# Attention and two expert layers on one core: the tokens of the smaller experts in two steps of four experts side by side instead of five steps of one

## The chip, the cores and the metric

The kernel runs on one core of one Trainium2 chip. The metric is the device time of one execution in microseconds (us); lower is better. The kernel before takes 847.58 us (median of three runs, 847.08 to 849.77).

## The reference

Three layers follow each other. All data are fp32.

```python
out_g = softmax(scale * q_g @ k_all.T) @ v_all        # 32 global tokens see all
out_l = softmax(global + windowed local scores) @ v   # 512 local tokens, window 32
x = concat(out_g, out_l) -> (4 * 544, 8 * 64) = (2176, 512)

h = x @ w_in                                          # 512 -> 2048
g = where(h >= 1, h, where(h <= -1, 0, (h + 1) ** 2 / 4))
x = g @ w_out                                         # 2048 -> 512

logits = normalised(x) @ normalised(expert_emb).T / tau      # 8 experts
expert_idx = argmax(logits); gate = softmax(logits)[expert_idx]
out[n] = gate[n] * (relu(x[n] @ w1[e]) @ w2[e])       # e = expert_idx[n], 512 -> 1024 -> 512
```

With these inputs 2091 of the 2176 tokens choose the same expert. Five others get 10, 15, 57, 1 and 2 tokens, and two get none. The kernel finds this out on the chip.

## The kernel before, in words

**Stages.** Attention runs first, with the weights of the first layer loaded and split beside it. Then the first layer is done for 17 tiles of 128 tokens in six blocks (3, 3, 2, 3, 3 and 3 tiles). Each block has 16 slots; a slot computes 128 of the 2048 hidden columns (`up1`, line 730), applies g (`act1`) and, two slots later, adds the slot's share of the output (`down1`, line 773). An fp32 matrix product is made of three matmuls of a reduced type, fp32r: each operand is split by a copy on ACT and a subtraction on DVE into a high part (names ending in h) and a low part (names ending in l), and high by high, high by low and low by high are added up in PSUM.

**Routing.** When a block's output is there, its tiles are routed in `pieces`: `logits` (line 637, eight passes of DVE over 512 columns for each tile), `choose` (lines 646 to 650: the maximum and `ohot`, the one-hot choice), and `route3` (lines 661 to 685: small matmuls `rk` count for each token how many tokens before it chose the same expert, and DVE then makes from this rank `ohlo`, a one-hot row of rank modulo 128, and `rhf`, rank divided by 128). After the fifth block `pick` takes the expert with most tokens so far, the large expert.

**The second layer** is a loop over 48 slots (six blocks of eight; the loop at line 1322, and I number these slots 0 to 47). A slot makes 128 of the 1024 hidden columns of one block for the large expert (`e_up`, line 1195: 12 matmuls of 384 columns), pops up to two routing pieces of the last block, and makes the share of the output that belongs to two slots earlier (`e_down`, line 1217: 9 matmuls of 512 columns). All tokens go through the large expert; those of other experts are dropped when the result is written. After a block's last slot, DVE multiplies each output tile by its gates into `ob` (line 1224, two buffers), and POOL writes it with an indirect DMA (line 1225). Each such write waits until the one before has landed, since they write the same tensor. What runs beside the loop is put into it by hand with `hook(slot, function)`; the functions of a slot run at its end, after `e_down`.

**The small experts.** When all tokens are counted (`count`, line 786), a chain of DVE operations (`members`, `steps1`, `steps1b`, `steps_e`, `steps_e2`) places the tokens of the other experts in steps of 128 places. A step belongs to one expert, so five experts make five steps. `place` (line 888) then turns the one-hot rows into a list of token numbers by 17 small matmuls (`li`, and later `gi` for the gates); `digits` (line 879) prepares their operands. Slots 10 to 13 hold this. Step j starts at slot 14 + 7j: `gather` fetches 128 rows (line 1098, POOL's queue), the 4 MB of the expert's weights are loaded in eight DMAs of 512 KB (lines 1051 and 1053, SP's queue; from the second step on a DMA is skipped if the expert is that of the step before), `split_T` transposes the rows (line 1082), `split_w` splits each weight piece (ACT line 1057, DVE line 1060), `up` and `down` multiply (line 1092, 24 matmuls of 512 columns each), and `put` scales (line 1118) and writes the rows (line 1119, POOL's queue). Five steps fit into the loop (`NS1 = 5`); further ones stand behind a test (line 1378) and don't run with these inputs.

Of the kernel before, what the change touches and what calls it, by code (L numbers as in the profile page):

```python
# [31 lines left out]
def kernel(  # L32
# [30 lines left out]
    NSTEP = NTILE + E + 1  # L63
# [36 lines left out]
    rki = const.tile([P, NTILE], I32, name="rki")  # L100
    rhf = const.tile([P, NTILE], F32, name="rhf")
    rlo = const.tile([P, NTILE], I32, name="rlo")
    rlof = const.tile([P, NTILE], F32, name="rlof")
# [551 lines left out]
    def route3(i, n):  # L655
# [9 lines left out]
        if i + n < NTILE:  # L665
# [6 lines left out]
        sl = slice(i, i + n)  # L672
        rkf = mp.tile([P, 3], F32, name="rkf", tag="rkf")[:, :n]
        nc.vector.tensor_reduce(out=rkf, in_=rt[:, :n], axis=AX.X, op=ALU.add)
        nc.vector.tensor_copy(out=rki[:, sl], in_=rkf)
        nc.vector.tensor_scalar(out=rlo[:, sl], in0=rki[:, sl], scalar1=P - 1, scalar2=None, op0=ALU.bitwise_and)
        nc.vector.tensor_copy(out=rlof[:, sl], in_=rlo[:, sl])
        nc.vector.tensor_tensor(
            out=ohlo[:, sl, :], in0=iota.unsqueeze(1).to_broadcast([P, n, P]),
            in1=rlof[:, sl].unsqueeze(2).to_broadcast([P, n, P]), op=ALU.is_equal,  # L680
        )
        nc.vector.tensor_scalar(
            out=rlo[:, sl], in0=rki[:, sl], scalar1=7, scalar2=None, op0=ALU.logical_shift_right
        )
        nc.vector.tensor_copy(out=rhf[:, sl], in_=rlo[:, sl])
# [77 lines left out]
    def down1(g):  # L763
# [12 lines left out]
        if f == KF - 1:  # L776
            B_.y = [y_out(t0 // P + i, B_.yp[i]) for i in range(nt)]
            ty.extend((t0 // P + i, y) for i, y in enumerate(B_.y))
            n = 2 if bi == 1 else 3
            rq.extend((pieces if bi != NB - 2 else pieces_last)(*[ty.pop(0) for _ in range(n)]))  # L780
# [7 lines left out]
    def pieces(*ty):  # L788

        (ta, ya), (tb, yb) = ty[:2]  # L790
        if len(ty) == 2:
# [11 lines left out]
            ]  # L803
        r = [lambda e=e: logits(ta, ya, e, e + 2) for e in range(0, E, 2)]
        r.extend([
# [5 lines left out]
        ])  # L811
        td, yd = ty[2]
        return r + [
# [5 lines left out]
            lambda: choose(td, 1),  # L819
            lambda: count(route3(td, 1)),  # L820
# [24 lines left out]
    NS1 = 5  # L845
# [28 lines left out]
    def digits(oh, t1, n, dig):  # L874

        nd = dig.shape[1]
        rl = rp.tile([P, t1, nd, n], BF16, name=f"rl{nd}", tag="rl")
# [85 lines left out]
    def steps1():  # L963

        ti = rp.tile([P, E], I32, name="ti")
        nc.vector.tensor_scalar(out=ti, in0=R["cnt"], scalar1=float(P - 1), scalar2=None, op0=ALU.add)
        nc.vector.tensor_scalar(out=ti, in0=ti, scalar1=7, scalar2=None, op0=ALU.logical_shift_right)
# [12 lines left out]
    def steps1b():  # L980
# [7 lines left out]
        nc.vector.tensor_tensor(out=stp, in0=stp, in1=rhf, op=ALU.add)  # L988
        nc.vector.scalar_tensor_tensor(
            out=stp, in0=mem, scalar=float(2 * NSTEP), in1=stp, op0=ALU.mult, op1=ALU.add  # L990
        )
        R["ohhi"] = ohhi = rp.tile([P, NTILE, NSTEP], BF16, name="ohhi")
        nc.vector.tensor_tensor(
            out=ohhi,
            in0=iota[:, :NSTEP].unsqueeze(1).to_broadcast([P, NTILE, NSTEP]),
            in1=stp.unsqueeze(2).to_broadcast([P, NTILE, NSTEP]),
            op=ALU.is_equal,
        )
        R["rl"] = digits(ohhi, NTILE, NSTEP, rdig)

    def steps2():
        li = ps.tile([P, 512], F32, name="li", tag="T")
        place(R["rl"], li[:, : 2 * NSTEP])
        R["idg"], R["ids"] = id_list(li[:, : 2 * NSTEP], NSTEP, "")

    def steps_e():

        tot = rp.tile([1, 1], F32, name="tot")
        R["tot"] = tot
        nc.vector.tensor_reduce(out=tot, in_=R["tf"][0:1], axis=AX.X, op=ALU.add)  # L1010
        en = rp.tile([1, E], F32, name="en")
        nc.gpsimd.tensor_tensor(out=en, in0=R["sta"][0:1], in1=R["tf"][0:1], op=ALU.add)
        jt = rp.tile([1, NSTEP], F32, name="jt")
# [72 lines left out]
    def mm3(dst, ah, al, wsel, nch, mid=None):  # L1086
        for c in range(nch):
            if mid and c == nch - 2:
                mid()
# [332 lines left out]
```

## Time and profile before

| | us |
|---|---|
| median of three runs | 847.58 |
| the profiled execution: its own time | 847.4 |
| the profiled execution: its span, first to last instruction | 845.2 |
| TensorE (PE) busy within the span | 792.9 |
| DVE, ACT, POOL busy | 576.4, 445.2, 153.1 |

The span is shorter than the time by 2.2 us, which lie around it. In the rows of the profile, PE is the matmul part of TensorE and PEld its weight loads; DVE, ACT and POOL are the vector, scalar and general engines; SP issues most DMAs. A row of the timeline gives the start, the duration, the engine, the line, and out<-in of equal neighbours put together ("x4"). The duration of a matmul runs until its result has left the array, and the next one starts before that: what a matmul costs is the distance from its start to the next start. "PEclk" or "clock" is the granted share of the TensorE clock.

### The profile page before, as it was taken

To read this page: it belongs to the slowest core of one execution; us is meant where nothing else is said; L and a number is where in the kernel's file an instruction comes from. 1 tells how busy PE (TensorE), PEld (TensorE's weight loads), DVE (VectorE), ACT (ScalarE), POOL (GpSimd) and SP (SyncE) were. 2 spreads that over 40 slices of the span, in tenths; PEclk is the share of its full clock that TensorE was granted. 3 is DMA by queue.
4 is the path that set the end of the run, shared out by engine and by line. 5 is a ranking of instruction groups with operands and counts; after the bars stand their busy time and mean duration, and the time that the engine had idled before them with its cause. 6 is when DMAs were issued, how large, how long until landed. Compare 5 with 4: busy or idle time off the path is not lost. (4 is left out here: it accounts for less than half of the span.)

```text
span 845.2 us, 14802 instructions
## 1 busy us (share of the span) xinstructions
PE 792.9 (94%) x5135; PEld 687.8 (81%) x5135; DVE 576.4 (68%) x1675; ACT 445.2 (53%) x1060; POOL 153.1 (18%) x310
## 2 busy tenths in 40 slices
PE   6989987899999999999999999989989999999993
PEld 4767666699899989999899888978878888888782
DVE  4888997788957789767777878768564645353422
ACT  2989986555655557656556556632113533333230
POOL 4777885502000000000000000100111010010201
PEclk6989998899999999999999999999999999999997
DMA  7677787533330020000010023121135616072400
GB/s 187 196 208 210 201 220 218 188 101 126 102 136 1 1 76 1 28 36 1 0 63 2 1 88 100 63 88 38 38 92 194 238 48 228 26 275 70 146 0 35
DMA packets 68049, 86.00 MB, mean 102 GB/s; under 512 B 26832, under 2 KB 47312, under 8 KB 67968
## 3 DMA queue, kind: packets, MB, share of 16 engines
q1 hardware_dynamic: 65808, 79.22, 30.1%
q0 software_dynamic: 2160, 5.77, 2.0%
q8 instruction: 42, 0.69, 0.3%
q14 instruction: 39, 0.32, 0.1%
HBM read 67.98 MB, written 14.43 MB: 98 GB/s over the span
## 5 line engine op out<-in xcount | busy, mean ns | idle before, releaser
L730 PE MATMUL hps<-xh,winh 128*128 128x384 f32 (+1 forms) x384 | 126.4, 329 | 0.0
L730 PE MATMUL hps<-xl,winh 128*128 128x384 f32 (+1 forms) x384 | 126.2, 329 | 0.0
L730 PE MATMUL hps<-xh,winl 128*128 128x384 f32 (+1 forms) x384 | 125.8, 327 | 0.0
L773 PE MATMUL yp<-woh,gh 128*128 128x512 f32 x272 | 107.6, 396 | 0.5 <-DVE y L610 0.4
L773 PE MATMUL yp<-wol,gh 128*128 128x512 f32 x272 | 107.3, 394 | 0.0
L1201 DVE SCALAR_TENSOR_TENSOR el<-eh,eg 128x384 fp32r<-128x384 f32 (+1 forms) x48 | 25.5, 532 | 82.9 <-ACT eg L1200 82.9
L730 PEld LDWEIGHTS hps<-xh,winh 128*128 128x128 f32 x384 | 72.6, 189 | 4.0
L730 PEld LDWEIGHTS hps<-xh,winl 128*128 128x128 f32 x384 | 72.5, 189 | 3.8
L1200 ACT ACTIVATE eg<-eh 128x384 fp32r<-128x384 f32 (+1 forms) x48 | 22.7, 473 | 96.0 <-PE eh L1195 96.0
L730 PEld LDWEIGHTS hps<-xl,winh 128*128 128x128 f32 x384 | 72.4, 188 | 0.0
L760 DVE TENSOR_TENSOR wol<-wof,woh 128x512 fp32r<-128x512 f32 x96 | 66.4, 691 | 1.2
L1195 PE MATMUL eh<-exh,wh 128*128 128x384 f32 (+1 forms) x192 | 65.5, 341 | 1.3 <-ACT exh L1083 1.3
L1195 PE MATMUL eh<-exl,wh 128*128 128x384 f32 (+1 forms) x192 | 63.8, 332 | 1.0 <-DVE exl L1084 1.0
L1195 PE MATMUL eh<-exh,wl 128*128 128x384 f32 (+1 forms) x192 | 63.6, 332 | 0.0
L926 POOL TENSOR_TENSOR gt<-ssq,half 128x14 f32<-128x14 f32 (+1 forms) x2 | 3.6, 1824 | 326.6 <-ACT jk L619 326.6
L1060 DVE TENSOR_TENSOR wl<-rw,wh 128x1024 fp32r<-128x1024 f32 x48 | 56.8, 1220 | 3.8 <-ACT wh L1057 3.6
L773 PEld LDWEIGHTS yp<-woh,gh 128*128 128x128 f32 x272 | 51.2, 188 | 9.1 <-DVE y L610 1.4
L460 ACT ACTIVATE sm<-sm,st 128x160 f32<-128x160 f32 x128 | 53.4, 426 | 9.0 <-DVE st L450 9.0
L759 ACT CAST woh<-wof 128x512 fp32r<-128x512 f32 x96 | 58.0, 605 | 0.1
L773 PEld LDWEIGHTS yp<-wol,gh 128*128 128x128 f32 x272 | 51.2, 188 | 8.0
L482 POOL TENSOR_SCALAR pn<-sm,st 128x128 f32<-128x128 f32 x128 | 53.4, 434 | 17.9 <-DVE st L478 8.0
L1217 PE MATMUL eo<-wh,eg 128*128 128x512 f32 x136 | 53.7, 395 | 1.9 <-DVE ob L1224 1.9
(915 smaller groups left out, 1924.0 us busy)
## 6 DMA issues: line engine op xcount, KB each, us to landing
rw<-in_moe_w SPq DMA_DIRECT2D x48, 512.0 KB, 7.1
raw<-in_moe_w_in SPq DMA_DIRECT2D x16, 512.0 KB, 6.8
raw<-in_moe_w_out SPq DMA_DIRECT2D x16, 512.0 KB, 5.1
k<-in_k_l SPq DMA_DIRECT2D x16, 256.0 KB, 5.4
q<-in_q_l SPq DMA_DIRECT2D x16, 256.0 KB, 5.4
xsc<-xs SPq DMA_DIRECT2D x16, 256.0 KB, 5.6
ysc<-y SPq DMA_DIRECT2D x16, 256.0 KB, 2.5
ye<-ysc SPq DMA_DIRECT2D x16, 256.0 KB, 3.3
```

Source lines behind the costliest of these rows:

```text
L460: nc.scalar.activation(out=sm[:, i, :], in_=sm[:, i, :], func=AF.Exp, scale=-1.0, bias=st[:, 0, i : i + 1], accum_out=st[:, 1, i : i + 1],)
L482: eng_of[AT["f4"][i]].tensor_scalar(out=pn[:, i, :].rearrange("p (c x) -> p c x", c=2), in0=sel(sm[:, i, :]), scalar1=st[:, 2, i : i + 1], ...
L730: nc.tensor.matmul(hp_[:, :n], lhsT=wt[:, kk, fs], rhs=xt, start=kk == 0 and i == 0, stop=kk == KD - 1 and i == 2)
L759: nc.scalar.copy(out=woh, in_=wof[f // 2][:, f % 2, :])
L760: nc.vector.tensor_tensor(out=wol, in0=wof[f // 2][:, f % 2, :], in1=woh.bitcast(F32), op=ALU.subtract)
L773: nc.tensor.matmul(B_.yp[i], lhsT=gt[:, cs], rhs=wt, start=f == 0 and k == 0, stop=f == KF - 1 and k == 2)
L926: nc.gpsimd.tensor_tensor(out=gt[:, 0, sl], in0=ssq[:, sl], in1=half.to_broadcast([P, t1 - t0]), op=ALU.pow)
L1060: le.tensor_tensor(out=l, in0=raws[c], in1=h.bitcast(F32), op=ALU.subtract)
L1195: nc.tensor.matmul(hps[:, :n], lhsT=w[:, fs], rhs=x, start=kk == 0 and i == 0, stop=kk == KD - 1 and i == 2)
L1200: nc.scalar.activation(out=gh, in_=hps[:, :n], func=AF.Relu)
L1201: nc.vector.scalar_tensor_tensor(out=gl, in0=hps[:, :n], scalar=0.0, in1=gh.bitcast(F32), op0=ALU.max, op1=ALU.subtract)
L1217: nc.tensor.matmul(B_.yp[i], lhsT=a[:, cs], rhs=w, start=f == 0 and k == 0, stop=f == KF2 - 1 and k == 2)
```

## The change

The steps of the small experts are built anew. A step still has 128 places, but they are four groups of 32 (`QW = 32`), and each group belongs to an expert of its own. The 85 tokens make six groups (the expert with 57 tokens has two), which are two steps. For each of 16 parts of a step's weights (`NSUB`: eight for the first matrix, eight for the second), four matmuls write 32 partitions each of the same PSUM tile `qo`: the stationary operand is 32 columns of the transposed rows, the moving one the 128x512 weights of that group's expert, in fp32 as they come from memory. The weights are no longer split, so the copies on ACT and subtractions on DVE for them are gone. In the trace of before a matmul of this kind is recorded as two.

The 32 parts of the two steps go one to a slot, from slot 14 to slot 45 (`T0`, `T1`), each three slots after the issue of its four DMAs of 256 KB, which are skipped where the group is empty. The weights of six groups are 24 MB, where five steps loaded 20 MB; the second step has two empty groups.

The list is made differently. `route3` keeps only the rank (`rkf`), and `ohlo` is made at once for all 17 tiles in `steps1b`, since place and rank now shift together. The routing of the last block has its own pieces (`pieces_end`, seven instead of sixteen), of which one is popped in a slot; `choose` and `route3` of the last tile, which shared a slot, stand in neighbouring slots. The count then falls into slot 8 instead of 9, and the chain into slots 9 to 11 instead of 11 to 13. `steps_e` works on 76 groups instead of 26 steps, and its two POOL multiplications are on DVE.

At the end, `ob` has three buffers for the large expert and one for the steps; the middle tile of a block is scaled by ACT. The last two slots' `e_down` are done tile by tile, so that each tile is finished and written before the next. The split of the large expert's weights and the load and transposes of the second block are some slots earlier. The core of the diff:

```diff
-    NSTEP = NTILE + E + 1
+    QW = 32
+    NQ4 = P // QW
+    NSTEP = -(-(NTOK // QW + E) // NQ4)
+    NQ = NQ4 * NSTEP
...
-        nc.vector.tensor_copy(out=rki[:, sl], in_=rkf)
...
-        nc.vector.tensor_copy(out=rhf[:, sl], in_=rlo[:, sl])
+        nc.vector.tensor_reduce(out=rkf[:, i : i + n], in_=rt[:, :n], axis=AX.X, op=ALU.add)
...
+    def pieces_end(*ty):
+
+        (ta, ya), (tb, yb), (td, yd) = ty
+        return [
+            lambda: (logits(ta, ya, 0, 4), ysq(ta, ya)),
+            lambda: (logits(ta, ya, 4, 8), logits(tb, yb, 0, 1)),
+            lambda: (choose(ta, 1), logits(tb, yb, 1, 5), ysq(tb, yb)),
+            lambda: (route3(ta, 1), logits(tb, yb, 5, 8), choose(tb, 1)),
+            lambda: (logits(td, yd, 0, 4), ysq(td, yd)),
+            lambda: (route3(tb, 1), logits(td, yd, 4, 8), choose(td, 1)),
             lambda: count(route3(td, 1)),
         ]
...
-    NS1 = 5
+    NS1 = 2
...
+    class Quad:
...
+        def load(self, s):
+            n = NSUB * self.j + s
+            for p in range(2):
+                t = self.raw[s, p] = raws[(2 * n + p) % NC].rearrange("p (i d) -> p i d", i=2)
+                for i in range(2):
+                    ev, ch = self.e[2 * p + i]
...
+                    nc.sync.dma_start(out=t[:, i, :], in_=src.rearrange("e p f -> (e p) f"), cond=ch)
+
+        def mm(self, s):
...
+            a, c = (self.yT, s % KD) if s < 2 * KD else (self.hT, s - 2 * KD)
+            ws = [self.raw.pop((s, p)) for p in range(2)]
+            for i in range(NQ4):
+                cs = slice(QW * i, QW * (i + 1))
+                nc.tensor.matmul(self.o[cs], lhsT=a[:, c, cs], rhs=ws[i // 2][:, i % 2, :], start=first, stop=last)
...
-                ob = rp.tile([P, DM], F32, name="ob", tag=f"ob{(t + 1) % 2}")
-                nc.vector.tensor_scalar(out=ob, in0=B_.yp[i], scalar1=gt[:, 1, t : t + 1], scalar2=None, op0=ALU.mult)
+                ob = rp.tile([P, DM], F32, name="ob", tag=f"ob{1 + t % 3}")
+                if i % 2:
+                    nc.scalar.activation(out=ob, in_=B_.yp[i], func=AF.Copy, scale=gt[:, 1, t : t + 1])
...
-        hook(4, lambda: (gates(0, TE), members(0, TE)))
-        hook(10, close_mp, lambda: norms(TE, NTILE))
-        hook(11, lambda: (gates(TE, NTILE), members(TE, NTILE), steps1()))
-        hook(12, steps1b, steps_e)
-        hook(13, steps_e2, steps2)
+        hook(6, lambda: (gates(0, TE), members(0, TE)))
+        hook(9, lambda: (members(TE, NTILE), steps1(), steps1b()))
+        hook(10, steps_e)
+        hook(11, steps2, lambda: norms(TE, NTILE))
+        hook(11, lambda: quads[0].regs(0, NQ4))
+        hook(12, quads[0].gather, lambda: gates(TE, NTILE))
+        hook(13, quads[0].trans)
...
+        T0, T1 = 14, 46
...
+            (j, s), q = divmod(n, NSUB), T0 + (T1 - T0) * n // (NS1 * NSUB)
+            hook(q - 3, lambda r=r, s=s: r.load(s))
+            hook(q, lambda r=r, s=s: r.mm(s))
...
+        for i in range(blocks[NB - 1][1]):
+            e_down(NES - 2, [i])
+            e_down(NES - 1, [i])
```

On PE, before, this stands in the first half of the first step, between the large expert's `eo` of one slot and its `eh` of the next (h is the step's hidden part, wh and wl the split weights, yTh and yTl the split rows):

```order
L1217 MATMUL eo_7657<-wh_7274,el 128x512
L1092 MATMUL h_8047<-wh_7940,yTh 128x512
L1092 MATMUL h_8047<-wl_7941,yTh 128x512
L1092 MATMUL h_8047<-wh_7940,yTl 128x512
L1092 MATMUL h_8047<-wh_7944,yTh 128x512
L1092 MATMUL h_8047<-wl_7945,yTh 128x512
```

Six more of this kind follow before the next `eh`. Of the change, this stands between two slots (rw is the unsplit weights, hTh the transposed hidden part):

```order
L1199 MATMUL eo_8021<-wl_7089,eg 128x512
L1199 MATMUL eo_8021<-wh_7088,el 128x512
L1133 MATMUL qo<-rw_6397,hTh 32x512 x2
L1133 MATMUL qo<-rw_6484,hTh 32x512 x2
L1109 MATMUL qt<-ident,hb 128x128 x4
L1177 MATMUL eh<-exh,wh_6574 128x256
```

Four matmuls of 32 partitions stand in every slot from 14 to 45, where up to 24 of 128 partitions stood in some. On DVE, before, the chain of the list runs in slots 12 and 13 (ohhi is the one-hot step, rl the operand of `li`, ge the comparison that finds each step's expert):

```order
L983 TENSOR_TENSOR sel<-ohot,sta 128x136
L987 TENSOR_REDUCE stp<-sel 128x17
L988 TENSOR_TENSOR stp<-stp,rhf 128x17
L989 SCALAR_TENSOR_TENSOR stp<-mem,stp 128x17
L993 TENSOR_TENSOR ohhi<-iota,stp 128x442
L879 TENSOR_TENSOR rl_7780<-ohhi,rdig 128x17x26 x2
```

Of the change, from slot 9 on:

```order
L995 CAST pf_7538<-pi_7535 128x34
L998 TENSOR_TENSOR ohlo<-iota,pf_7538 128x2176
L998 TENSOR_TENSOR ohhi<-iota,pf_7538 128x323
L1183 SCALAR_TENSOR_TENSOR el<-eh,eg 128x384
L1012 TENSOR_REDUCE tot<-tf 1x1
L1014 TENSOR_TENSOR en<-sta,tf 1x8
L1017 TENSOR_SCALAR ge<-iota,tot 1x76
L1022 TENSOR_TENSOR ge<-ge,sta 1x608
L1022 TENSOR_TENSOR ge<-ge,en 1x608
L1026 TENSOR_TENSOR ge<-ge 1x608
```

The large comparison that makes `ohlo` and the whole of `steps_e` now stand ahead of the operands of `li` (`rl`), which come later in this row.

More of the change, by code (lines that the diff above doesn't have):

```diff
@@ L1008, in steps_e @@
         tot = rp.tile([1, 1], F32, name="tot")
-        R["tot"] = tot
         nc.vector.tensor_reduce(out=tot, in_=R["tf"][0:1], axis=AX.X, op=ALU.add)
         en = rp.tile([1, E], F32, name="en")
-        nc.gpsimd.tensor_tensor(out=en, in0=R["sta"][0:1], in1=R["tf"][0:1], op=ALU.add)
-        jt = rp.tile([1, NSTEP], F32, name="jt")
+        nc.vector.tensor_tensor(out=en, in0=R["sta"][0:1], in1=R["tf"][0:1], op=ALU.add)
+        ge_ = rp.tile([P, 2 * DM], F32, name="ge", tag="hTl")[0:1]
+        jt, ex = (ge_[:, (E + k) * NQ : (E + k + 1) * NQ] for k in range(2))
@@ L1084, in split_T @@
         nc.vector.tensor_tensor(out=l, in0=t, in1=h.bitcast(F32), op=ALU.subtract)
[L1086 to L1089, printed above, removed]
-            wh, wl = wsel(c)
-            for k, (a, w) in enumerate(((ah, wh), (ah, wl), (al, wh))):
-                nc.tensor.matmul(
-                    dst, lhsT=a[:, c, :], rhs=w, start=c == 0 and k == 0, stop=c == nch - 1 and k == 2
-                )
     def gather(idg, j):
@@ L1146, in split, with tr @@
-        def split(self, *cs):
-            for c in cs:
-                self.w[c] = split_w(c, *w_tiles(c), nc.scalar, nc.vector)
-        def up(self, f):
-            self.hb = up2(self.yh, self.yl, [self.w[c] for c in range(KD)], f)
+            self.yT = rp.tile([P, KD, P], F32, name="yTh")
+            self.tr(self.y, self.yT)
+            self.hT = rp.tile([P, KF2, P], F32, name="hTh")
+        def tr(self, src, dst):
+            t = ps.tile([P, 4, P], F32, name="qt", tag="T")
+            for kk in range(4):
+                nc.tensor.transpose(t[:, kk, :], src[:, kk * P : (kk + 1) * P], ident)
+            nc.scalar.copy(out=dst, in_=t)
@@ new lines, in mm @@
+        def mm(self, s):
+            first, last = (s % KD == 0, s % KD == KD - 1) if s < 2 * KD else (s == 2 * KD, s == NSUB - 1)
+            if first:
+                self.o = ps.tile([P, 512], F32, name="qo", tag="T")
+            a, c = (self.yT, s % KD) if s < 2 * KD else (self.hT, s - 2 * KD)
[3 more added lines that the diff above has]
+                nc.tensor.matmul(self.o[cs], lhsT=a[:, c, cs], rhs=ws[i // 2][:, i % 2, :], start=first, stop=last)
+            if last and s < 2 * KD:
+                self.hb = rp.tile([P, 512], F32, name="hb")
+                nc.scalar.activation(out=self.hb, in_=self.o, func=AF.Relu)
@@ L1204, in e_up, with e_down @@
         eq[q] = gh, gl
-    def e_down(q):
+    def e_down(q, tiles=None):
         b, f = divmod(q, KF2)
@@ L1211, in e_down @@
             B_.yp = [ps.tile([P, DM], F32, name=f"eo{i}", tag="y", bufs=3) for i in range(nt)]
-        gh, gl = eq.pop(q)
+        gh, gl = eq[q]
         wh, wl = [w[:, (f % 2) * DM : (f % 2 + 1) * DM] for w in wA[KD + f // 2]]
-        for i in range(nt):
+        for i in range(nt) if tiles is None else tiles:
             cs = slice(i * P, (i + 1) * P)
@@ L1343 @@
                     x_split(bi + 1, [(f - 9) // 2])
-            for _ in range(1 if g < nsl else 2):
-                if rq:
-                    rq.pop(0)()
+            if rq:
+                rq.pop(0)()
             if g < nsl:
```

241 lines of the change are left out of this document (104 added, 137 removed).

## The prediction

> **What bounds the kernel now.** I first read the busy time of each engine by stages. This is the second layer; the columns are the stage, its length, PE, PEld, DVE, ACT and POOL busy, the clock, the DMA share and GB/s.
>
> ```profile
> core 0: us, PE busy (x) PEld busy (x) DVE busy (x) ACT busy (x) POOL busy (x), PEclk, DMA share, GB/s
> 640.00:700.00 60.00, 60.00 (x332) 52.65 (x331) 30.47 (x41) 23.56 (x37) 7.95 (x8) 1.00 0.39 138
> ...
> 780.00:820.00 40.00, 38.05 (x186) 32.97 (x185) 15.52 (x20) 10.69 (x16) 4.95 (x5) 1.00 0.25 79
> 820.00:845.20 25.20, 10.64 (x49) 8.33 (x47) 8.14 (x9) 4.37 (x5) 3.93 (x4) 0.77 0.08 29
> ```
>
> PE is busy without a gap at full clock where the small experts' steps run; DVE and ACT are half idle. So this stage is worth what it takes on PE, until the last stage, where PE stops early. Second, I read what PE waited for from 200 us on (total, times, longest).
>
> ```profile
> PE rk L661 <- DVE ohot L650: 3.5, 2, 2.0
> PE tt L1082 <- DMA yg<-ysc,idg: 2.1, 1, 2.1
> PE eo L1217 <- DVE ob L1224: 1.9, 1, 1.9
> ...
> PE li L888 <- DVE tot L1010: 0.9, 1, 0.9
> ```
>
> Three of them, 3.5 + 0.9 + 2.1 = 6.5 us, belong to the start of the small experts: the choice of a tile's expert, the list, and the first gather. Third, I read the timeline for distances.
>
> ```profile
> 805.94 0.40 PE L1092 MATMUL h<-wh,yTh 128*128 128x512 f32 x1
> ...
> 808.74 0.33 PE L1195 MATMUL eh<-exh,wh 128*128 128x384 f32 x1
> ...
> 810.85 0.39 PE L1217 MATMUL eo<-wh,eg 128*128 128x512 f32 x1
> ...
> 811.57 0.56 DVE L1201 SCALAR_TENSOR_TENSOR el<-eh,eg 128x384 fp32r<-128x384 f32 x1 [6.43 <-ACT eg L1200]
> ...
> 812.93 0.60 PE L1082 MATMUL tt<-ident,hb 128*128 128x128 f32 x4
> 813.28 0.48 PE L1092 MATMUL h<-wh,yTh 128*128 128x512 f32 x1
> ```
>
> Twelve matmuls of a step take 808.74 - 805.94 = 2.80 us, 0.233 each. A slot of the large expert takes 812.93 - 808.74 = 4.2 us, and four transposes take 0.35. The slot's `el` starts 2.8 us after the slot.
>
> **Removed from PE.** 5 steps x 48 = 240 matmuls:
>
> ```profile
> 600.00:845.20 245.20, 59.04 (x240) 44.41 (x240) 0.97 0.34 120
> ```
>
> This row is line 1092 alone; its 59.0 us hold the tails under which the next work starts, so I take 240 x 0.233 = **-55.9 us**. Of 15 groups of four transposes (line 1082: one for a step's rows, two for its hidden part) 6 are left: 9 x 0.35 = **-3.2 us**. The 40 splits of weights leave DVE and ACT; PE did not wait for them, so this counts only at the end, below.
>
> **Added to PE.** The new matmul is in the trace already: attention's global scores (line 391) multiply 32 stationary columns by 512 moving ones in plain fp32, four of them into four quarters of the partitions of one tile.
>
> ```profile
> 31.83 0.71 PE L534 MATMUL pv<-ptB,vgz 128*128 128x128 f32 x4
> 32.47 1.08 PE L391 MATMUL sg<-kw,qgz 128*32 128x512 f32 x8
> 33.35 0.26 PE L392 MATMUL sg<-kw,qgz 128*32 128x32 f32 x8
> 33.55 0.37 PE L438 MATMUL s<-kw,qT 64*64 64x160 f32 x4
> ```
>
> Eight records are four matmuls, two passes each. They take 33.35 - 32.47 = 0.88 us together, while one record alone lasts about 0.6: the four run side by side. Around them the shape used of the array changes. Into it: the last of the four L534 started near 32.27 (row end 32.54 less its 0.27), so the step into 32 columns took 0.20 where its neighbours follow at 0.11 to 0.15. Out of it: L392's last started near 33.42, and the next shape came 0.13 later. I take 0.2 us for both changes: 32 parts x 1.08 = **+34.6 us**. The Trainium skill speaks against the change here: "TensorEngine Tiling (Array Packing)", Tiling Modes, says that a change of the mode drains TensorE. The rows agree that there is a price, and they put it at about 0.1 us.
>
> **The start of the small experts.** DVE decides it, and here are its prices.
>
> ```profile
> 577.56 0.69 DVE L637 SCALAR_TENSOR_TENSOR jk<-y,ebchTl 128x512 bf16<-128x512 f32 x1
> 578.17 0.69 DVE L1084 TENSOR_TENSOR exl<-tt,exh 128x512 fp32r<-128x512 f32 x1
> 578.78 0.17 DVE L935 TENSOR_SCALAR gt<-gt 128x14 f32<-128x14 f32 x1
> ...
> 582.55 0.17 DVE L922 TENSOR_TENSOR ide<-rid,big 128x14 uint32<-128x14 int32 x1
> 582.64 0.55 DVE L1201 SCALAR_TENSOR_TENSOR el<-eh,eg 128x384 fp32r<-128x384 f32 x1
> ```
>
> ```profile
> 601.65 0.29 DVE L678 TENSOR_TENSOR ohlo<-iota,rlof 128x128 bf16<-128x128 f32 x1
> ```
>
> ```profile
> 621.03 0.62 DVE L993 TENSOR_TENSOR ohhi<-iota,stp 128x442 bf16<-128x442 f32 x1
> 621.68 1.15 DVE L879 TENSOR_TENSOR rl<-ohhi,rdig 128x442 bf16<-128x442 bf16 x2
> ...
> 623.19 0.36 DVE L1019 TENSOR_TENSOR ge<-jt,sta 1x208 bf16<-1x208 f32 x1
> ```
>
> One `logits` pass is 0.61 us, `gates` with `members` 3.9 (578.78 to 582.64), an `el` 0.5, a small operation 0.17 to 0.19. From 128 to 442 elements a comparison goes from 0.29 to 0.62, 1.05 ns an element; so `ohlo` at 2176 elements is 2.4 us and `ge` at 608 about 0.8.
>
> First wait: in slot 6 `el` ends 3.3 us into the slot; four logits 2.4, gates and members 3.9, el 0.5, route 0.5, four logits 2.4 and a choice 0.8 follow, so the last choice is there 13.8 us after slot 6's start. On PE the route's `rk` stands behind two slots and the third's up part, 2 x 4.2 + 2.1 = 10.5, with some 0.2 for a route's small matmuls 10.7. PE waits 3.1 us.
>
> Second wait: from `el` of slot 9, 2.8 us into it, DVE has four el (1.9), two ob (1.5, a 0.75 each in the last rows below), members (0.7), steps1 (1.3), steps1b (4.5 with ohlo), steps_e (4.9: four ge, a reduction like them, and small ones), exl (0.6) and two digits at 323 elements (0.9): 16.3 us. The `li` matmuls stand at the end of slot 11, 3 x 4.2 and a group of transposes, 13.0 us after slot 9's start. PE waits 2.8 + 16.3 - 13.0 = 6.1 us. What is queued behind it on PE is slot 12; DVE has no need of that. The gather is asked for behind the list as before, but its transposes stand two slots later, 8.7 us after the list (two slots and a group of transposes); the row of its DMAs gives 4.2 us in the median:
>
> ```profile
> yg<-ysc,idg POOLq DMA_INDIRECT x5, 4.2
> ```
>
> I cost it at nothing.
>
> So 9.2 us of waits stand where 6.5 were: +2.7. A wait also costs clock:
>
> ```profile
> 595.00:600.00 5.00, 3.43 (x18) 1.00 0.00 0
> 600.00:605.00 5.00, 4.60 (x18) 0.67 0.01 2
> ```
>
> After the wait of 2.0 us the clock was 0.67 for 5 us, a loss of 1.6. I take one such loss more, since both new waits are longer: **+4.3 us** for the start. Its ends: with all waits gone -6.5 - 1.6 = -8.1; with DVE 3 us later than I count, +7.
>
> **The weights.** Four DMAs a slot, 1.05 MB. SP's timeline and a stage of before in which weights flow:
>
> ```profile
> 656.37 6.17 SPq L1053 DMA_DIRECT2D rw<-in_moe_w  x8
> ```
>
> ```profile
> 664.00:668.00 4.00, 4.00 (x23) 3.40 (x23) 0.00 (x0) 0.00 (x0) 0.00 (x0) 1.00 1.05 406
> ```
>
> An issue takes 0.77 us, four 3.1; at 406 GB/s the megabyte takes 2.6. A slot with its part takes 4.2 + 1.08 = 5.3 us, and the DMAs are asked for three slots ahead. I cost them at nothing; without this cover it would be the second rival.
>
> **The end.** POOL's writes and PE's last matmul:
>
> ```profile
> 828.11 0.98 POOL L1225 DMA_INDIRECT out<-ob,ide  x1 [29.85 <-DVE ob L1224]
> ...
> 830.25 0.39 PE L1092 MATMUL ops<-wh,hTl 128*128 128x512 f32 x1
> 831.57 0.75 DVE L1224 TENSOR_SCALAR ob<-eo,gt 128x512 f32<-128x512 f32 x1 [3.07 <-PEq L1378]
> 832.25 0.98 POOL L1225 DMA_INDIRECT out<-ob,ide  x1 [3.15 <-DMA out<-ob,ide]
> 835.76 0.98 POOL L1225 DMA_INDIRECT out<-ob,ide  x1 [2.53 <-DMA out<-ob,ide]
> 839.10 0.98 POOL L1119 DMA_INDIRECT out<-ob,ids  x1 [2.36 <-DVEq L1378]
> ```
>
> PE ends at 830.6, and the span 14.6 us later. Four writes follow each other at 3.3 to 4.1 us, and the last needs 6.1 us to the end of the span. More buffers don't loosen this chain: the writes still wait for each other. But now three writes are in it, and the first tile is ready two tiles (12 x 0.233 = 2.8) before PE's end: -2.8 + 0.9 for ob, two distances of 3.7, then 6.1 make 11.6 us. **-3.0 us**. The wait of `eo` for `ob`, **-1.9 us**, goes with the third buffer; nothing is late next there, since a tile's buffer is then free for a whole block.
>
> **The sum.** The profiled execution took 847.4 us, within 0.2 of the median. 847.4 - 55.9 - 3.2 + 34.6 + 4.3 - 3.0 - 1.9 = 822.3: **822 us**.
>
> **The rivals.** *Two by two, or in turns* (slower than before). In the four scores of line 391 two matmuls share a moving tensor; here each has its own, and each waits for its own DMA. If they ran two at a time, a group would take 2 x 0.88 us: 32 x 0.88 = +28 gives 850; wholly in turns +85 gives 907. The point where the gain is gone is a group of 0.88 + 25.1/32 = 1.66 us. For it speaks that no row shows four sources; against it, that four stationary operands and two sources cost no more than one matmul's two passes.
>
> *Side by side in part.* If the four lose a third to each other, which the scores with their two sources don't show, a group takes 1.17 us and the sum is 32 x 0.29 = 9 higher: 831. The Trainium skill, "TensorE: Matmul & The Clock Gate", Part 3, measured 3.07 times for four row tiles and 2.38 times for three column tiles; by the former a group would be 4 x 0.88 / 3.07 = 1.15 us. The trace doesn't bear that out: its four take what two passes of one take.
>
> *The weights come late* (also slower). If they came only at the 138 GB/s that the stage from 640 to 700 us had on the mean, each of the first step's 16 slots would take 7.6 us instead of 5.3: 16 x 2.3 = +37, 859. Against it stand the 406 GB/s, and that this mean holds pauses.
>
> *The start doesn't wait.* If DVE keeps up in slots 5 to 11, the start gains 8.1 instead of losing 4.3: 810.
>
> **How the numbers follow.** Forecast 0.66; the start without waits 0.14; side by side in part 0.07; two by two or in turns 0.06; weights late 0.05; else 0.02. About the forecast the terms move it: mode changes of 0.1 us or of 0.6 (if the array's 0.2 us tail and a weight load show) are -3 to +13, the start -12 to +3, the end 2 either way. The range is 809 to 837. About 0.3% (2.5 us) is what a measurement of this kernel tells from no change. Faster 0.92, same 0.02, slower 0.06.
>
> **What would show it.** Right: rows of `qo` x8 of about 1.1 us, 32 times; no PE wait for weights; `rk` waiting about 3 us and `li` about 6; three writes after PE's end. Wrong: `qo` records that start 0.4 us apart within a group, PE waiting for `rw`, or a last stage as long as before.

## The result, and the profile after

The changed kernel takes 817.57 us (median of four runs, 814.89 to 820.61); the kernel before, beside it on the same chip, 847.33 (four runs, 844.75 to 849.77). The ratio is 0.965, with a 95% interval of 0.9606 to 0.9695. The profiled execution took 820.61 us, with a span of 818.9. A repeat of the changed kernel on another chip (e11_again, below) gave 818.95 (813.08 to 819.15).

I read the same views as before the change. First the busy time by stages, with the columns of the first fence of the prediction:

```profile
core 0: us, PE busy (x) PEld busy (x) DVE busy (x) ACT busy (x) POOL busy (x), PEclk, DMA share, GB/s
640.00:700.00 60.00, 60.00 (x373) 42.31 (x371) 11.02 (x20) 12.61 (x25) 5.98 (x6) 1.00 0.78 261
700.00:740.00 40.00, 40.00 (x227) 29.08 (x220) 8.05 (x13) 6.67 (x13) 3.93 (x4) 1.00 0.39 119
```

PE is still without a gap where the small experts run, so this stage is still worth what it takes on PE. DVE's share has fallen from 30.47 of 60 us to 11.02 and ACT's from 23.56 to 12.61, which buys nothing here. What has grown is the load of the DMA engines: 0.78 in the first step, where it was 0.39. Next, what PE waited for:

```profile
PE li L886 <- DVE rl L877: 5.2, 1, 5.2
PE rk L661 <- DVE ohot L650: 3.1, 1, 3.1
```

Of the five waits shown before, `tt` for its gather and `eo` for `ob` are gone, two waits of `rk` have become one, and the one for the list has grown from 0.9 to 5.2. No weight is waited for. The timeline of PE around one of the 32 parts:

```profile
721.09 0.40 PE L1199 MATMUL eo<-wh,el 128*128 128x512 f32 x1
721.42 1.07 PE L1133 MATMUL qo<-rw,yTh 128*32 128x512 f32 x8
722.41 0.45 PE L1177 MATMUL eh<-exh,wh 128*128 128x384 f32 x1
722.70 0.34 PE L1177 MATMUL eh<-exh,wl 128*128 128x384 f32 x1
722.87 0.33 PE L1177 MATMUL eh<-exl,wh 128*128 128x384 f32 x1
...
726.78 1.06 PE L1133 MATMUL qo<-rw,yTh 128*32 128x512 f32 x8
```

Eight records in 1.07 us are the four matmuls side by side. A slot with its part takes 726.78 - 721.42 = 5.36 us, against 4.19 without one (808.74 to 812.93 in the prediction's rows): a part costs 1.18 us. Of that, 0.99 pass until the next matmul starts; about 0.1 lies ahead, since the step into the part is 0.33 where `eo` otherwise follow at 0.23; and about 0.1 behind, since the first `eh` is 0.29 from the next where the others are 0.17. The row of this line alone, for busy time by stages, answers to the 240 matmuls of before with 59.0 us:

```profile
600.00:818.90 218.90, 34.09 (x256) 5.04 (x256) 0.97 0.45 150
```

It has the 32 x 8 records. The end of the kernel, with POOL's writes:

```profile
805.35 0.98 POOL L1211 DMA_INDIRECT out<-ob,ide  x1 [8.82 <-DVE ob L1208]
809.06 0.98 POOL L1211 DMA_INDIRECT out<-ob,ide  x1 [2.72 <-DMA out<-ob,ide]
812.55 0.98 POOL L1211 DMA_INDIRECT out<-ob,ide  x1 [2.51 <-DMA out<-ob,ide]
```

and PE's last matmul:

```profile
806.62 0.39 PE L1199 MATMUL eo<-wh,el 128*128 128x512 f32 x1
```

Three writes are left instead of four, and the first starts 1.7 us ahead of PE's end at 807.0. From there to the end of the span it is 11.9 us, where it was 14.6. To see where the rest of the gain lies, I take the second layer's first and last matmul on PE. The first is, in the timeline of before,

```profile
552.04 0.44 PE L1195 MATMUL eh<-exh,wh 128*128 128x384 f32 x1 [1.33 <-ACT exh L1083]
```

and in that of the changed kernel

```profile
550.47 0.44 PE L1177 MATMUL eh<-exh,wh 128*128 128x384 f32 x1 [1.33 <-ACT exh L1060]
```

The layer shrank on PE from 830.6 - 552.0 = 278.6 us to 807.0 - 550.5 = 256.5, by 22.1, and the tail by 2.7. The other 1.5 us lie ahead of the layer. In the traces of the changed kernel and its variants the layer starts between 545.7 and 550.5 us, though the work ahead of it is the same in all of them; with one trace of before, its 552.0 can't be told from such differences between executions. So below, small differences are compared by the length of the second layer on PE (first `eh` to the end of the last matmul) rather than by medians. This table is worked out for all profiled runs in that way; tail is from there to the end of the span. Layer and tail are those of the one profiled execution, the median is of all runs of the kernel, so the two need not move together. The last two columns are the half-clock stretches behind the two waits, for the last section.

| kernel | median us | layer | tail | `rk` wait | `li` wait | half clock behind `rk` | behind `li` |
|---|---|---|---|---|---|---|---|
| before | 847.33 | 278.6 | 14.6 | 1.6, 2.0 | 0.9 | 0, 3.4 | 0 |
| after | 817.57 | 256.5 | 11.9 | 3.1 | 5.2 | 6.8 | 3.4 |
| e1_turns | 897.91 (one run) | 336.5 | 12.0 | 3.1 | 5.3 | 0 | 6.8 |
| e2_digits_first | 811.55 | 247.0 | 11.8 | 3.1 | none | 0 | 0 |
| e3_gates_later | 813.75 | 251.5 | 11.9 | 0.4 | 5.2 | 0 | 6.8 |
| e4_fours | 818.16 | 252.9 | 12.0 | 3.1 | 5.2 | 6.8 | 3.4 |
| e5_both | 806.34 | 244.3 | 12.0 | 0.4 | none | 0 | 0 |
| e6_pairs | 801.17 | 239.4 | 12.1 | 0.4 | none | 0 | 0 |
| e7_end_whole | 819.62 | 254.6 | 14.1 | 3.1 | 5.2 | 0 | 6.8 |
| e8_two_ob | 820.09 | 259.7 | 12.3 | 3.1 | 7.7 | 6.8 | 6.8 |
| e9_ring_two | 819.93 | 257.0 | 12.0 | 3.1 | 5.2 | 0 | 6.8 |
| e10_ring_one | 841.59 (one run) | 279.2 | 12.1 | 3.1 | 5.2 | 0 | 6.8 |
| e11_again | 818.95 | 256.5 | 12.2 | 3.1 | 5.3 | 6.8 | 3.4 |

### The profile page after: what moved, and what is told of

Same layout as the page of the kernel before. It is cut to its first block, busy times and chain, and to the rows that moved or that the text cites. A ratio compares the mean times of both kernels' runs of the same rounds, so it can differ in the third digit from the quotient of the medians.

```text
span 818.9 us, 14821 instructions
## 1 busy us (share of the span) xinstructions
PE 767.8 (94%) x5115; PEld 641.6 (78%) x5115; DVE 505.3 (62%) x1513; ACT 404.2 (49%) x1011; POOL 146.6 (18%) x301
## 5 line engine op out<-in xcount | busy, mean ns | idle before, releaser
L1177 PE MATMUL eh<-exh,wh 128*128 128x384 f32 (+1 forms) x192 | 67.7, 353 | 1.3 <-ACT exh L1060 1.3
L1211 POOL DMA_INDIRECT out<-ob,ide x17 | 19.3, 1134 | 210.9 <-DVE ob L1208 178.0
L482 POOL TENSOR_SCALAR pn<-sm,st 128x128 f32<-128x128 f32 x128 | 53.3, 434 | 18.9 <-DVE st L478 10.7
L1177 PEld LDWEIGHTS eh<-exh,wh 128*128 128x128 f32 x192 | 36.9, 192 | 24.7 <-issue 19.3
```

The lines of the kernel that those rows point to most:

```text
L482: eng_of[AT["f4"][i]].tensor_scalar(out=pn[:, i, :].rearrange("p (c x) -> p c x", c=2), in0=sel(sm[:, i, :]), scalar1=st[:, 2, i : i + 1], ...
L1177: nc.tensor.matmul(hps[:, :n], lhsT=w[:, fs], rhs=x, start=kk == 0 and i == 0, stop=kk == KD - 1 and i == 2)
L1211: nc.gpsimd.indirect_dma_start(out=out, out_offset=bass.IndirectOffsetOnAxis(ap=ide[:, t : t + 1], axis=0), in_=ob, in_offset=None, bounds ...
```

## The experiments

The theory is the prediction's: four matmuls side by side cost about what one costs, a part is paid on PE alone, and the two waits at the start are DVE's. Against each stands a rival: the four share something, the weights or the array's change of shape sets the price, or the waits have another cause.

**In turns (e1_turns).** Do the four really run side by side, and what is that worth? All four matmuls of a part write one quarter, which turns with the part.

```diff
-                nc.tensor.matmul(self.o[cs], lhsT=a[:, c, cs], rhs=ws[i // 2][:, i % 2, :], start=first, stop=last)
+                to = slice(QW * (s % NQ4), QW * (s % NQ4 + 1))
+                nc.tensor.matmul(
+                    self.o[to], lhsT=a[:, c, cs], rhs=ws[i // 2][:, i % 2, :], start=i == 0, stop=i == NQ4 - 1
+                )
```

> The four matmuls of a part all write to the same 32 partitions (the quarter changes from part to part), so that they cannot run side by side; the small experts' outputs are not the reference's here. My theory: the change gains because the four run at once in 0.88 us. Taken in turns they cost 4 x 0.88 = 3.5 us a part, 32 x 2.65 = 85 us more: about 903 us, slower than before, and PE without waits for weights. The rival, that the gain comes from elsewhere (no splits of weights on DVE and ACT, the end, the start) and that the array's columns are not what matters: within 10 us of the changed kernel, about 820.

One run took 897.91 us. PE's timeline:

```profile
746.85 3.62 PE L1134 MATMUL qo<-rw,yTh 128*32 128x512 f32 x8
750.40 0.44 PE L1180 MATMUL eh<-exh,wh 128*128 128x384 f32 x1
...
754.77 3.62 PE L1134 MATMUL qo<-rw,yTh 128*32 128x512 f32 x8
```

The same eight records now take 3.55 us to the next matmul instead of 0.99, and a slot 7.92 instead of 5.36. Within the row the records start 0.43 apart; in the changed kernel the first four start within 0.02 us and the second four 0.45 later. So the four, with four sources of their own, run side by side in full: two passes of 0.43 to 0.45 us, whether one matmul makes them or four. The Trainium skill, "TensorE: Matmul & The Clock Gate", Part 3, gives 3.07 times for four row tiles and 2.38 for three column tiles; eight passes of 0.43 in 0.88 us are 3.9 times here (3.55 / 0.99 = 3.6 with the way in and out), and the measurement decides for this form. The layer grew by 336.5 - 256.5 = 80.0 us. By the rows the side by side is worth 32 x (3.55 - 0.99) = 81.9; 2 us of it are hidden because this execution lost less clock at the start (see the table).

**The digits first (e2_digits_first).** Is the `li` wait made by DVE's work ahead of the list? `digits` of the list stands ahead of `steps_e`, which the list does not need; the transposes and all parts move a slot later, to 15 to 46.

```diff
-        R["rl"] = digits(R["ohhi"], NTILE, NSTEP, rdig)
...
-        hook(10, steps_e)
+        hook(10, lambda: R.update(rl=digits(R["ohhi"], NTILE, NSTEP, rdig)), steps_e)
...
-        hook(13, quads[0].trans)
+        hook(14, quads[0].trans)
...
-        T0, T1 = 14, 46
+        T0, T1 = 15, 47
```

> The operands of the token list are made ahead of steps_e (slot 10) instead of behind it, and the parts stand one slot later (15 to 46), the transposes of the gathered rows too. My theory: the 5.2 us that PE waits for the list are DVE's queue, of which steps_e is 4.9: the wait falls under 1 us and a clock loss of up to 1.6 us goes with it, 811 to 814 us where the changed kernel has 817.6. The rival, that DVE's time only moves (the list's last part then comes behind steps_e, and the gather is late): a new wait of 3 to 5 us for the gathered rows or the first weights, no gain.

It took 811.55 us (809.2 to 812.73), ratio to the kernel before 0.959 (0.956 to 0.962). Of the waits of PE at the start, one is left:

```profile
PE rk L661 <- DVE ohot L650: 3.1, 1, 3.1
```

The layer lost 9.5 us, 5.2 of them the wait itself. The rest is clock: no half-clock stretch is left in it. Of these 4.3 us, 2.8 were lost behind `rk` in the changed kernel (worked out in the last section); the `rk` wait is as long here and merely was not followed by a drop, so these 2.8 are not this edit's.

**Gates later (e3_gates_later).** The same for `rk`: `gates` and `members`, 3.9 us of DVE that nobody needs yet, go two slots later, behind the routing.

```diff
-        hook(6, lambda: (gates(0, TE), members(0, TE)))
+        hook(8, lambda: (gates(0, TE), members(0, TE)))
```

> gates and members of the first 14 tiles go from slot 6 to slot 8, behind the last choice. My theory: the 3.1 us that PE waits for the last tile's choice are DVE's 3.9 us of gates in front of it; the wait goes, and the gates fall into the time in which DVE waits for slot 9. 813 to 815 us. The rival, that the chain of the list is pushed back by as much: the wait for the list grows from 5.2 to 8 us, no gain.

It took 813.75 us (811.58 to 813.99), ratio 0.9612 (0.9585 to 0.9639).

```profile
PE li L886 <- DVE rl L877: 5.2, 1, 5.2
PE rk L661 <- DVE ohot L650: 0.4, 1, 0.4
```

`rk` waits 0.4 instead of 3.1 us, and the list does not come later for it. The layer lost 5.0: 2.7 of wait, and the rest is clock, 2.8 less lost behind `rk` and a little more behind `li`.

**Both (e5_both).** The two edits together.

> Both moves at the start of the small experts together: the digits of the list come ahead of the steps of the list in DVE's order (as in the run with the digits first), and gates and members stand two slots later (as in the run with the gates later). Each alone shortened the second layer on PE, from 256.5 us in the changed kernel to 247.0 and to 251.5. Theory (two separate waits, each with its own work on DVE in front of it): the gains add, no rk wait over 0.5 us and no li wait, second layer 242 to 244 us, median about 807. Rival (the waits are one lack of DVE time, which shows at whichever place comes next): gates and members, now in the way of the list, bring back an li wait of 2 us or more; second layer 246 to 250, median 810 to 814.

It took 806.34 us (804.08 to 807.58), ratio 0.9533 (0.9511 to 0.9555).

```profile
PE rk L661 <- DVE ohot L650: 0.4, 1, 0.4
```

The layer is 244.3, 12.2 less than the changed kernel's; the two alone lost 9.5 + 5.0 = 14.5. They add, but for the clock lost behind `rk`, 2.8 us in the changed kernel (worked out in the last section), which is missing in both and can be saved once. Put together anew, 12.2 is the two waits (5.2 and 2.7) and the 4.3 us of clock lost behind them. The rival, a wait that comes back elsewhere, falls.

**Four parts at a time (e4_fours).** What does the change of shape cost? The parts stand four together in every fourth slot.

```diff
-            (j, s), q = divmod(n, NSUB), T0 + (T1 - T0) * n // (NS1 * NSUB)
+            (j, s), q = divmod(n, NSUB), 17 + 4 * (n // 4)
```

> The 32 parts stand four at a time in the slots 17, 21 and so on to 45, instead of one in each slot from 14 on. A part costs 1.18 us in its slot (5.37 against 4.19 us without), of which 0.88 are its four matmuls. My theory: the other 0.3 are the two changes of the array's shape, so that 24 of 32 pairs of changes fall away, less a few for the transposes between: 5 to 7 us less, 811 to 813 us. The rival, that the 0.3 are the matmuls' own (their weight loads, or the waits for four DMAs): no change, 818. If weights come in bursts of 4 MB too late: PE waits of some us at the slots 17, 21, 25, and slower.

It took 818.16 us (817.07 to 818.81), ratio 0.9666 (0.9638 to 0.9693): no different from the changed kernel. The forecast time of 811 to 813 was missed. In the profiled execution, the fastest of the four, the layer is 3.6 us shorter than that of the changed kernel, with the same half-clock stretches, and would be 6.1 shorter, as the theory had it, but for a new wait of 2.5. By PE's timeline a slot with four parts takes 7.86 us, and the one behind it 4.27 instead of 4.19, since its first `eh` is late; so a part takes (7.86 + 0.08 - 4.19) / 4 = 0.94 instead of 1.18. The rival, that the 0.3 belong to each part, falls. The row with the wait:

```profile
661.40 0.63 PE L1059 MATMUL tt<-ident,ye 128*128 128x128 f32 x4 [2.55 <-DMA ye<-ysc]
```

This is a transpose of the large expert's rows. SP's timeline says why they were late:

```profile
643.95 11.61 SPq L1123 DMA_DIRECT2D rw<-in_moe_w  x16
655.67 0.55 SPq L1157 DMA_DIRECT2D ye<-ysc  x1
```

The load of `ye` stood behind 16 loads of weights on SP's queue, and these took 11.6 us to issue.

**Pairs (e6_pairs).** Both moves at the start, and the parts two by two, with half the queue's burst.

```diff
-            (j, s), q = divmod(n, NSUB), T0 + (T1 - T0) * n // (NS1 * NSUB)
+            (j, s), q = divmod(n, NSUB), T0 + 2 * (n // 2)
...
-            if s in (KD, 2 * KD):
+            if s in (KD + 1, 2 * KD + 1):
```

> As the kernel with both moves, and the parts stand two together in every second slot, so that the array changes its shape 16 times instead of 32 on the way in and out; the transposes of the hidden part come behind the second part. Theory (a part costs 1.18 us of which some 0.35 is the way in and out, as four parts at a time have shown: 0.92 a part): 16 x 0.35 = 5 us less than the kernel with both moves, second layer about 238, a slot with two parts 4.19 + 2.0. Rival (the 8 loads in one go hold SP's queue, 8 x 0.77 = 6.2 us, and what else stands there comes late, as the transposed rows did for 2.5 us with four at a time): a PE wait for a DMA appears and no more than 1 us is gained.

It took 801.17 us (799.35 to 801.48), ratio 0.9464 (0.9445 to 0.9484): the best of all, with no wait for a DMA. A pair:

```profile
752.32 1.93 PE L1132 MATMUL qo<-rw,hTh 128*32 128x512 f32 x16
754.17 0.44 PE L1176 MATMUL eh<-exh,wh 128*128 128x384 f32 x1
```

Two parts take 1.85 us to the next matmul where two single ones take 2 x 0.99 = 1.98, and they save one way in and one first `eh` as well. The layer lost 244.3 - 239.4 = 4.9 us, 0.31 for each of 16 ways in and out saved; neither of the two has a half-clock stretch in it. Together with the four at a time, (4 x 1.18 - 3.75) / 3 = 0.32, this prices the way in and out at about 0.3 us. That all of it is the change of the array's shape is not shown. In the trace of before, behind four transposes that use the whole array (812.93 in the prediction's rows), the first matmul, at 813.28, also starts its neighbour late:

```profile
813.60 0.39 PE L1092 MATMUL h<-wl,yTh 128*128 128x512 f32 x1
813.83 0.39 PE L1092 MATMUL h<-wh,yTl 128*128 128x512 f32 x1
```

It is 0.32 from the next where the others are 0.23. So of the 0.1 behind a part, most comes without a change of shape as well.

**The end whole (e7_end_whole).** The last two `e_down` are written one behind the other, as before the change.

```diff
-        for i in range(blocks[NB - 1][1]):
-            e_down(NES - 2, [i])
-            e_down(NES - 1, [i])
+        e_down(NES - 2)
+        e_down(NES - 1)
```

> The changed kernel with the last two down parts of the large expert written whole, one behind the other, instead of tile by tile. Theory (the tail is the chain of three writes, which starts when the first tile is ready): the first tile is ready 2 x 3 matmuls before PE's end instead of 2 x 6, so the stretch from PE's last matmul to the end grows by 1.4 us, from 11.9 to 13.3; all else alike, 819. Rival (POOL's earlier writes set when the chain starts): 11.9 as it is.

It took 819.62 us (816.24 to 820.88); the tail is 14.1 instead of 11.9.

```profile
802.95 0.98 POOL L1211 DMA_INDIRECT out<-ob,ide  x1 [10.18 <-DVE ob L1208]
807.36 0.98 POOL L1211 DMA_INDIRECT out<-ob,ide  x1 [3.43 <-DMA out<-ob,ide]
```

PE ended at 803.24, so the first write started 0.3 us ahead of it instead of 1.7: the 1.4 expected. Another 0.7 is that this write was followed by the next after 4.41 us instead of 3.71; why it landed later, these runs don't say. The layer is 2 us shorter than the changed kernel's, which is again clock behind `rk`.

**Two output buffers (e8_two_ob).** Two buffers for the large expert's `ob`, and no tile scaled by ACT, as before the change.

```diff
-                ob = rp.tile([P, DM], F32, name="ob", tag=f"ob{1 + t % 3}")
-                if i % 2:
+                ob = rp.tile([P, DM], F32, name="ob", tag=f"ob{1 + t % 2}")
+                if False:
```

> The changed kernel with two output buffers instead of three and all output tiles written by DVE, as before the change. Theory (eo waited 1.9 us for ob in the kernel before because of the two buffers): that wait is back, 1.5 to 2.5 us on PE, and the tail grows by up to 0.4 where one of its tiles waits its turn on DVE: second layer 258 to 259 us, 819 to 820. Rival (the buffers come free in time in the new order, since the last block is written tile by tile): no such wait, 817 to 818.

It took 820.09 us (818.66 to 822.24). `eo` waits again, but only 0.5 us; the surprise is the wait of `li`:

```profile
PE li L886 <- DVE rl L877: 7.7, 1, 7.7
...
PE eo L1199 <- DVE ob L1208: 0.5, 1, 0.5
```

DVE's timeline has the reason:

```profile
603.05 0.75 DVE L1208 TENSOR_SCALAR ob<-eo,gt 128x512 f32<-128x512 f32 x1 [2.82 <-DMA out<-ob,ide]
```

With two buffers, the third tile of a block must wait until the first is written. DVE stands still for 2.8 us, right in the chain that leads to the list, and the list is 2.5 us later. So the third buffer is worth less at the place where it was missing before than at the start of the small experts, which the change had made tight. The layer is 3.1 us longer (259.67 against 256.54). The forecast of 819 to 820 us was met, but by luck: the wait that makes it stands elsewhere.

**Weights for two parts, and for one (e9_ring_two, e10_ring_one).** How near is the rival of the late weights? The weights have buffers for four parts; here for two, and for one (in brackets).

```diff
-                t = self.raw[s, p] = raws[(2 * n + p) % NC].rearrange("p (i d) -> p i d", i=2)
+                t = self.raw[s, p] = raws[(2 * n + p) % 4].rearrange("p (i d) -> p i d", i=2)
...
-            hook(q - 3, lambda r=r, s=s: r.load(s))
+            hook(q - 2, lambda r=r, s=s: r.load(s))
```

(For one part: `% 2` and `q - 1`.)

> The changed kernel with buffers for the weights of two parts instead of four (each part's four DMAs can start once the part two before it is done). Theory (the weights are never late because a part's megabyte needs about 3.3 us of issues, 12 issues having taken 9.95 us, and some 2 to 4 us to land, while a part comes every 5.4 us): two parts ahead give 9.7 us, so no PE wait for weights, 817 as the changed kernel. Rival (the four buffers are what hides them, and the margin is thin): PE waits for the weights in the first step, where the DMA share was highest, 10 us or more.

> The changed kernel with buffers for the weights of one part only: its DMAs start when the part before it is done, 4.3 us before its own turn. Theory (3.3 us of issues and 2 to 4 us to land): each of 31 parts waits 1 to 3 us, PE waits for the weights 30 to 95 us in all, 850 to 915; this is what the rival of late weights would look like, and how far the changed kernel is from it. Rival (the landing is faster than that, under 1 us): waits below 10 us in all, 820 to 828.

With two it took 819.93 us (816.45 to 820.48), as the changed kernel's repeat. The weight loads of PE, which come ahead of each matmul, show a small wait:

```profile
PEld qo L1133 <- DMA rw<-in_moe_w: 2.1, 4, 0.9
```

Nearly all of it is in two slots of the first step (6.14 and 5.10 us where the changed kernel has 4.45 and 4.46). The theory's "no wait" was wrong by 2 us, the rival's 10 by more. One of the forecast's terms was misread: the row of 9.95 us (SP's timeline of the changed kernel, from 643.03) holds eight issues, not twelve, with a pause of 5.2 us in the middle. The issues of one part follow at 0.69 us, so its four take 2.7 us, not 3.3. With one it took 841.59 us (one run), between the two guesses: the waits of PE for the weights are

```profile
PE qo L1133 <- DMA rw<-in_moe_w: 7.0, 6, 3.4
```

and those of its weight loads

```profile
PEld qo L1133 <- DMA rw<-in_moe_w: 18.9, 23, 4.3
```

together 26, and nearly all in the first step, where another half-clock stretch of 6.8 us stands behind the longest of them. In the second step, whose two empty groups halve the loads, slots mostly stay at 5.36 us even so: there the loads land within the 4.2 us that one slot gives. So the forecast's cover is real: with buffers for one part it costs 279.2 - 256.5 = 23 us, and two of the four are spare but for 2 us.

**Again (e11_again).** The changed kernel, unaltered.

> The changed kernel once more, unaltered, on another chip: what a repeat of the same kernel gives, against which the small differences of the other runs stand. Theory: 815 to 821, rk wait 3.1 and li wait 5.2 again since DVE's work in front of them is the same; the clock lost behind the rk wait may be 2.8 us or none, since it was the one in the changed kernel and the other in the run with the end written whole. Rival (the clock drop behind the rk wait is fixed by the order of the work): 2.8 us lost again.

818.95 us (813.08 to 819.15), ratio 0.9662 (0.9605 to 0.972); layer 256.5, waits 3.1 and 5.3, the same half-clock stretches. The rival's 2.8 us were lost again, but e7, e1, e2, e9 and e10, whose order of work is the same up to there, did not lose them: the order alone does not fix it (last section). Medians of the same kernel differ by 1.4 us, its layer by less than 0.1.

## Why the prediction was right, step by step

The forecast of 822 us was built on the profiled execution; that took 820.6 (the median, 817.57, is lower: the other three executions had a mean clock of 0.972 to 0.977 where this one had 0.970). The second layer lost exactly the 22.1 us that the terms make without the end (-55.9 - 3.2 + 34.6 + 4.3 - 1.9). That exactness is partly luck, since errors of both signs are in it; so is part of the total, to which the 1.5 us ahead of the layer contribute.

- **Removed, -55.9 and -3.2.** The steps' matmuls are gone from PE; counted from start to start in the trace of before they were 56.4 us, and the transposes fell by 2.9.
- **Added, +34.6.** The mechanism held: eight records in 0.88 us plus edges, 32 times. The size was off: the way in and out costs about 0.3 us, not 0.2, as the pairs and fours show. 32 x 1.18 = +37.8. Of the three edges in the rows above (0.1 ahead, 0.99 instead of 0.88, and 0.1 behind) I had the first and about the second. The third I overlooked: that the matmul behind also starts its neighbour later stands in the trace of before, in the row at 813.28 that I had read for something else.
- **The start, +4.3.** The `rk` wait was 3.1 as worked out: the last choice came 13.9 us after slot 6's start where I had 13.8, PE 10.8 where I had 10.7. The `li` wait was 5.2 instead of 6.1, because DVE needed less than the 16.3 us that I had summed. These are `el` of slot 9 and the digits:

```profile
600.54 0.56 DVE L1183 SCALAR_TENSOR_TENSOR el<-eh,eg 128x384 fp32r<-128x384 f32 x1 [7.23 <-ACT eg L1182]
615.12 0.88 DVE L877 TENSOR_TENSOR rl<-ohhi,rdig 128x323 bf16<-128x323 bf16 x2
```

From 600.54 to 616.00 it is 15.5 us: three `el` stand in it where I counted four (0.5), and `steps_e` took 4.4 us, not 4.9. The half clock behind `rk` made both this `el` and PE's way to the list 1.0 us late, which cancels; e7, without it, waits 5.2 too. With 8.3 - 6.5 = +1.8 of waits, and 4.3 us of clock lost (what e2 and e5 won beyond the waits) where the two stretches of before lost some 2.8, the start cost +3.3. The two edits e2 and e3 show the cause of the waits: take either work out of DVE's way, and its wait is gone but for 0.4 us.
- **The weights, 0.** No wait; e9 and e10 show the cover and its price.
- **The gather, 0.** Its DMAs took longer, 5.6 us in the median where I read 4.2, and the 8.7 us covered that.

```profile
yg<-ysc,idg POOLq DMA_INDIRECT x2, 5.6
```

- **`eo` for `ob`, -1.9.** Gone. That nothing else hung on the third buffer was wrong in the other direction: without it the list would be late (e8).
- **The end, -3.0.** It was -2.7: three writes, with PE's last matmul as worked out. e7 shows that the order by tiles makes 1.4 of it, or 2.3 with the slower write.

With the measured sizes the terms make -56.4 - 2.9 + 37.8 + 3.3 - 1.9 = -20.1 us in the layer, against -22.1 measured. Of these 2 us, 0.8 can be found in the trace of before: behind each group of transposes the first matmul starts its neighbour 0.09 late, and the steps had 15 such groups where 6 are left. The other 1.2 I can't assign.

Of the rivals, in turns is refuted as the case and confirmed as a price: forecast at 907, 85 above, measured at 897.91, with 82 more for the parts. Two by two and side by side in part are refuted by the 0.88 us of the eight records, and the weights were not late. The start without waits was not what happened, but e5 built it: forecast at 810, measured at 806.34.

## What to carry to other kernels

When small matrices with few rows wait on one another, put them side by side in column quarters of one PSUM tile: four plain fp32 matmuls with their own moving tensors took the time of one, and then the way into such a group and out of it (0.3 us a time) is what is left to save by grouping them, as far as the DMA queue's other work allows. Work that moves earlier makes the chain that feeds it tight: list what the engine does between the last input and the first use, and move out what the use does not need (here 12 us from two moves, 4.3 of them clock). A buffer added for one wait can be holding off another, so take it away again after the change to see what it does now.

## What was not expected of the hardware

The same wait cost clock in one execution and nothing in another. The granted clock (the column before the DMA share) in the stretch behind the `rk` wait of 3.1 us, in the changed kernel:

```profile
592.00:598.80 6.80, 6.24 (x20) 5.37 (x21) 1.21 (x7) 0.00 (x0) 0.00 (x0) 0.50 0.00 0
```

in its repeat, e11_again:

```profile
590.10:596.90 6.80, 6.12 (x20) 5.26 (x21) 1.33 (x8) 0.00 (x0) 0.00 (x0) 0.50 0.00 0
```

and in e7_end_whole, whose work is the same up to the end, behind `rk` and then behind `li`:

```profile
590.90:597.70 6.80, 6.80 (x37) 6.04 (x36) 2.09 (x7) 1.18 (x2) 0.24 (x1) 1.00 0.00 0
609.70:616.50 6.80, 5.06 (x31) 4.97 (x32) 2.50 (x9) 0.28 (x1) 1.38 (x2) 0.50 0.31 100
```

Of nine executions with this wait, four had 6.8 us of half clock behind it and five none. Where it struck, two slots took 9.45 + 5.16 us instead of 7.6 + 4.19, a loss of 2.8; where it did not, the stretch behind the longer `li` wait was 6.8 us in the four executions that have that wait, and otherwise 3.4 (6.8 again behind e8's 7.7). In the layer all stretches are 3.4 us or twice that. The rows of before, the second of them behind the wait of 2.0:

```profile
553.90:557.30 3.40, 3.40 (x15) 3.10 (x15) 0.00 (x0) 0.21 (x1) 0.00 (x0) 0.50 0.02 5
601.70:605.10 3.40, 3.40 (x11) 2.96 (x10) 1.85 (x6) 0.00 (x0) 1.25 (x1) 0.50 0.02 8
```

The first of them stands behind the two waits that open the layer, 1.3 and 1.0 us, which the changed kernel has too, without a drop. The traces tell hit from miss. Within one execution all changes of the clock lie on one grid of 3.41 us (to 2 ns), and where that grid lies against the work differs between executions. Divide the time at the grid, and look at the piece that ends where the drop starts, in the changed kernel and, for the wait of 2.0, before:

```profile
588.56:591.97 3.41, 0.91 (x6) 0.59 (x4) 3.31 (x15) 0.49 (x1) 0.00 (x0) 1.00 0.00 0
598.27:601.68 3.41, 1.44 (x10) 1.12 (x10) 2.01 (x12) 0.49 (x1) 0.00 (x0) 1.00 0.01 2
```

and at the two pieces over which the same wait of 3.1 us falls in e7, without a drop:

```profile
585.81:589.22 3.41, 1.89 (x11) 1.57 (x10) 3.27 (x15) 0.49 (x1) 0.00 (x0) 1.00 0.00 0
589.22:592.63 3.41, 1.84 (x12) 1.56 (x13) 2.15 (x13) 0.00 (x0) 0.00 (x0) 1.00 0.00 0
```

PE was busy for 0.91 and 1.44 us of a piece ahead of the drops, and for 1.89 and 1.84 where none came. Worked out in this way for the layer of all 13 traces, each of the 16 drops follows a piece in which PE was busy for 1.44 us or less, and no piece at full clock with 1.63 us or more was followed by one. So what counts is how much of a wait falls into one piece: e7's 3.1 us are divided into 1.5 and 1.6, and the two waits that open the layer fall into one piece before (2.3 us idle) and into two in the changed kernel. The Trainium skill, "TensorE: Matmul & The Clock Gate", Part 1, says that the clock is set by a window of about 3.4 us which runs on by itself; the grid agrees with that. It puts the drop behind a wholly idle window, and here the measurement decides: pieces that were idle for 2.0 of 3.4 us were followed by a drop. Since the kernel doesn't choose where the grid lies, a wait of a few us is to be priced with its clock as a chance: here 0 or 2.8 us on top of 3.1. The other surprise is how far one queue reaches: 16 weight loads, which the four parts at a time needed early, held up an unrelated load for 11.6 us.
